# Recall of a compressive memory: blocks of 128 features in fp32, or heads of 18 features as float16 pairs through DRAM

## The chip, the cores and the metric

The kernel runs on one core of a Trainium2 chip. A core has five engines that work side by side, each through its own queue of instructions in order: TensorE (PE, the matrix products, with its weight loads shown as PEld), VectorE (DVE), ScalarE (ACT), GpSimd (POOL) and SyncE (SP), which here issues every transfer (DMA). Data lie in SBUF (128 partitions), products are summed in eight banks of PSUM, and DRAM is reached by DMA alone. The metric is the device time of one execution in microseconds.

## The reference

A sequence of 2048 tokens of 576 features is cut into four segments of 512. Each of 32 heads has 18 features. A segment attends to itself causally, and it reads a memory M (18x18 for each head) with a sum z of the segments before it; phi is 1 + t above zero and exp(t) below. The result is mixed with a GEGLU network of 4608 hidden features.

```python
for s in range(N):
    logits = jnp.einsum("bhqd,bhkd->bhqk", qs, ks) * scale + mask
    a_dot = jnp.einsum("bhqk,bhkd->bhqd", _softmax(logits, axis=-1), vs)
    pq = phi(qs)
    num = jnp.einsum("bhld,bhde->bhle", pq, M)
    den = jnp.einsum("bhld,bhd->bhl", pq, z)[..., None] + 1e-6
    outs.append(g * (num / den) + (1.0 - g) * a_dot)
    pk = phi(ks)
    M = M + jnp.einsum("bhld,bhle->bhde", pk, vs)
    z = z + jnp.einsum("bhld->bhd", pk)
...
b = (_gelu(x @ w_gate) * (x @ w_up)) @ w_down
return sigmoid((x * gate_w).sum(-1)) * (o @ wo) + (1 - sigmoid(...)) * b
```

## The kernel before

Almost every product is done with float16 pairs: a number is split into a high word and the rest, a low word, and the product is the sum of high x high, high x low and low x high.

The first 210 us hold the projections and the memory, and the rest the network, the attention and the output. The loop at the end of the function's first part runs over four segments `s`. For `s` above 0 it begins with a **rows stage**: for each of four blocks `q` of 128 tokens two products make the values (`vrows`), `key_rows` turns the key features of the segment before (`p = s - 1`), `memorize` adds them to the memory in PSUM banks U and pv, and, from `p = 1` on, `recall(p, q)` reads the memory. Then come nine **products** `j` (`project`, 14 matmuls of 512 columns each): `j` 0 to 3 and half of 4 are queries, the rest keys. The results lie in banks dn (j = 0), st (two of them, j = 1, 2, 5, 6), U (3, 7) and G (4, 8); a bank is free again when ACT and DVE have read it, and the next product for that bank waits for that. `put_columns` writes the words of `j` one product later: ACT makes the high word (`stage`), a relu and an exp, DVE the low word and the other half of phi, POOL their sum, into `phi[s, j]`.

Recall before the change: five fp32 matmuls, one for each block of 128 features, against `bd`, an fp32 block matrix of the memory that has the heads on its diagonal; a head that lies across two blocks has two parts, which `put_recall` adds. `keep_memory(p)`, at j = 1, scales the memory in PSUM and masks it into `bd`. For the last segment the recalls come after products 6, 7 and 8.

Beside the products of segments 0 to 2 runs `next_x`: ACT squares the next segment's x, POOL and DVE add the squares, and at product `XJ` (5, 5, 4) `scale_x` has PE sum them over the partitions (`norm_x`); from this DVE makes the scale `xsc`, POOL the products of scales `al`, `nal`, `esc` (`outscale`), ACT the high words of x (`high_x`, products 5 to 7) and DVE the low ones (`low_x`, 6 to 8). The next rows stage begins with them. `form_sums` makes sums of x for the network.

The order of PE, ACT, DVE and POOL is that in which the program is written. `later` collects the second half of a step, which `finish_later` writes out after the product. SP's order is set by the compiler, and each of its transfers waits in line: a transfer that is not ready holds all behind it.

## Time and profile before

| | us |
|---|---|
| runs | 1557.70, 1557.97, 2040.06 |
| median | 1557.97 |
| the profiled execution | 1557.72 |
| its span, first to last instruction | 1555.6 |
| its granted TensorE clock | 1.00 |

A page of the profile gives the busy time of each engine, its share of the span in 40 slices, the DMA queues, the chain of work that ended last (followed back from the last instruction to what released it), and the costliest groups of instructions. A row of the timeline has the start in us, the duration in us of one instruction or of several merged (x10), the engine, the line, the operation, what it writes and reads with its shape, and in brackets the idle time before it and what ended that. Durations overlap on PE: the time that a group takes is the distance to the next start.

### The profile page before, as it was taken

The page shows a single profiled execution, that of the slowest core. Times are in us where ns is not written, and L with a number is a line of the kernel's source. Part 1 is how long each engine was busy: PE and PEld are TensorE (multiplying, and loading weights), DVE is VectorE, ACT ScalarE, POOL GpSimd, SP SyncE. Part 2 cuts the span into 40 slices and gives each one's busy share as a digit, 9 for nine tenths or more (in the row PEclk, how much of TensorE's full clock was granted, in tenths as well). Part 3 has the DMA queues.
Part 4 walks back from the last instruction along what each step waited for, and adds up shares of the span by engine and source line. Part 5 has one row for each costly group of instructions (what it writes and reads, how often), then busy time and mean ns, then how long its engine had stood idle before and what let it go on. Part 6 is the DMA issues. An engine that isn't in the chain of part 4 may idle for free.

```text
span 1555.6 us, 33618 instructions
## 1 busy us (share of the span) xinstructions
PE 1549.6 (100%) x12196; PEld 951.2 (61%) x12196; DVE 1263.4 (81%) x3255; ACT 1206.8 (78%) x2059; POOL 1129.0 (73%) x1219
## 2 busy tenths in 40 slices
PE   9999999999999999999999999999999999999999
PEld 5765755565656666656656565666656666656577
DVE  7878986878888888878788888888888888887665
ACT  7667544888888888888888888888888888887421
POOL 4354566768787868686877878786868687787597
PEclk9999999999999999999999999999999999999999
DMA  7744451555657576666656675757666665664635
GB/s 244 238 153 143 153 143 39 118 124 120 155 113 148 125 154 135 143 132 130 148 123 137 120 152 119 145 127 154 137 144 137 130 156 120 141 111 103 126 83 174
DMA packets 490966, 213.77 MB, mean 137 GB/s; under 512 B 427824, under 2 KB 469808, under 8 KB 490288
## 3 DMA queue, kind: packets, MB, share of 16 engines
q1 hardware_dynamic: 490800, 211.64, 59.8%
q8 instruction: 95, 1.56, 0.4%
q14 instruction: 71, 0.58, 0.1%
HBM read 90.99 MB, written 31.98 MB: 79 GB/s over the span
## 4 chain that ended last, share of the span: by engine, by line
PE 91%; POOL 4%; DMA 1%; DVE 1%; ACT 1%; SPq 0%; issue 0%; POOLq 0%; ACTq 0%
PE dn L1259 25%; PE U L531 17%; PE G L531 12%; PE V L531 6%; PE V L1379 5%; PE pv L1212 4%; PE st L412 3%; PE dn L419 2%; PE U L1305 2%; PE G L412 1%; PE U L412 1%; PE V L1310 1%; PE st L1174 1%; PE G L1310 1%; PE G L1305 1%; PE V L1305 1%
## 5 line engine op out<-in xcount | busy, mean ns | idle before, releaser
L531 PEld LDWEIGHTS <-pairg 128*128 128x128 f16 x2592 | 247.6, 98 | 257.3 <-issue 9.8
L1195 POOL TENSOR_TENSOR pl<-pb,ph 128x896 f16<-128x896 f32 (+1 forms) x128 | 185.7, 1472 | 211.5 <-ACT ph L1194 211.5
L1259 PE MATMUL dn<-paird,hhr 128*128 128x288 f16 x2115 | 328.8, 286 | 0.2 <-DVE acc L1267 0.2
L1193 ACT ACTIVATE pb<-pb,mb,esc 128x512 f32<-128x512 f32 (+3 forms) x512 | 304.9, 642 | 5.2
L1267 DVE SCALAR_TENSOR_TENSOR acc<-dn,ev,acc 128x288 f32<-128x288 f32 x533 | 262.7, 513 | 39.2 <-PE dn L1259 33.3
L1259 PEld LDWEIGHTS <-hhr 128*128 128x128 f16 x2160 | 206.8, 98 | 78.7 <-issue 11.8
L531 PE MATMUL G<-x,pairg 128*128 128x512 f16 x864 | 210.0, 379 | 0.2 <-DVE gl L1282 0.2
L531 PE MATMUL U<-xt,pairg 128*128 128x512 f16 x864 | 209.9, 379 | 0.0
L1259 PE MATMUL dn<-paird,hhd 128*128 128x288 f16 x1275 | 209.9, 286 | 0.0
L1195 POOL TENSOR_TENSOR pb<-pb,ph 128x896 f16<-128x896 f32 (+1 forms) x128 | 179.4, 1401 | 33.3 <-ACT ph L1194 27.7
L1194 ACT ACTIVATE ph<-pb 128x896 f16<-128x896 f32 (+1 forms) x256 | 188.6, 737 | 9.7
L345 POOL TENSOR_TENSOR pairg<-raw,pairg 128x384 f16<-128x384 f32 (+2 forms) x144 | 157.6, 1116 | 16.8 <-ACT pairg L341 16.8
L1177 DVE CUSTOM_DVE_ANT_0 pb<-st,mask 128x512 f32<-128x512 f32 (+1 forms) x256 | 157.3, 614 | 0.0
L1259 PEld LDWEIGHTS <-hhd 128*128 128x128 f16 x1296 | 123.8, 98 | 50.5 <-issue 6.5
L1177 DVE CUSTOM_DVE_ANT_0 pb<-dn,mask 128x256 f32<-128x256 f32 (+1 forms) x192 | 67.2, 375 | 64.6 <-PE dn L1174 62.9
L1379 PE MATMUL V<-xt,nest 128*128 128x256 f16 x714 | 105.5, 272 | 0.0
L531 PE MATMUL U<-x,pairg 128*128 128x512 f16 x432 | 105.0, 379 | 0.0
L531 PE MATMUL V<-x,pairg 128*128 128x512 f16 x426 | 103.8, 379 | 0.1
L1300 ACT ACTIVATE gl<-gl,sc 128x512 f32<-128x512 f32 x110 | 75.8, 715 | 34.1 <-DVE gl L1571 22.3
L1212 PEld LDWEIGHTS <-pt 128*128 128x128 f16 x2560 | 80.8, 96 | 13.2 <-issue 8.4
L1297 POOL TENSOR_TENSOR hhr<-gl,hhr 128x512 f16<-128x512 f32 x64 | 79.1, 1242 | 10.8 <-ACT hhr L1289 10.7
L1212 PE MATMUL pv<-vt,pt 128*128 128x37 f16 x2560 | 85.0, 179 | 0.0
(364 smaller groups left out, 3150.9 us busy)
## 6 DMA issues: line engine op xcount, KB each, us to landing
qkt<-qk SPq DMA_DIRECT2D x256, 108.0 KB
raw<-in_wgu_dram SPq DMA_DIRECT2D x36, 640.0 KB
rawd<-in_wd_dram SPq DMA_DIRECT2D x36, 288.0 KB
qk<-stage SPq DMA_DIRECT2D x32, 256.0 KB
qk<-stage SPq DMA_DIRECT2D x40, 128.0 KB
vp<-vstage SPq DMA_DIRECT2D x16, 296.0 KB
vt<-vp SPq DMA_DIRECT2D x16, 296.0 KB
orow<-oa SPq DMA_DIRECT2D x16, 288.0 KB
```

Of the source, the lines that this page charges most:

```text
L345: pool.tensor_tensor(spot(f, *p, 1), raw_g[f][:, p[0] : p[1]], spot(f, *p, 0), OP.subtract)
L412: pe.matmul(o, w(k, a), x[:, i], start=n == 0, stop=n == 13, skip_group_check=True)
L531: pe.matmul(o, w[:, i, (a + k) * P : (a + k + 1) * P], x[:, b + k], start=start and k == 0 and i == 0 and b == h, stop=k == 1 and i == 1, ...
L1177: dve.tensor_tensor_reduce(scored(a, qi), out[qi], mask[:, L - (qi + 1) * P :], 1.0, -3e38, OP.add, OP.max, mx[a][:, qi : qi + 1])
L1193: act.activation(r, r, AF.Exp, bias=b[:, qi : qi + 1], scale=esc[:, 0, c : c + 1])
L1194: act.activation(h[:, cols], p, AF.Copy)
L1195: pool.tensor_tensor(low[:, cols], p, h[:, cols], OP.subtract)
L1212: pe.matmul(ov, pr[:, 10 * i + COL[qi] // P + kb], v[:, 4 * e + kb, c0 : c0 + VC], start=kb == 0 and i == 0, stop=kb == qi and i == 1)
L1259: pe.matmul(o[:, :NH], hh[:, a, q * P : (q + 1) * P], w[:, b, n * NH : (n + 1) * NH], start=i == 0, stop=i == 5)
L1267: dve.scalar_tensor_tensor(av, o[:, :NH], ev, av, OP.mult, OP.add)
L1297: pool.tensor_tensor(hh[:, 1], t, hh[:, 0], OP.subtract)
L1379: pe.matmul(o, w[:, (7 * c + i) * P : (7 * c + i + 1) * P], x[d], start=start and n == 0, stop=n == 2, skip_group_check=True)
```

## The change

Recall goes by heads and with float16 pairs.

- `put_columns` scales phi by a power of two of its own (`ali`, and a bias `lnv` in the exp; the scale had been applied in `key_rows`). `split_phi` then makes a pair of each query block of 128 features: ACT copies it to float16, POOL subtracts, and SP writes it to DRAM (`phq`) as three rows for each feature, high, low, high.
- `load_phi(s, g)` reads 54 rows (18 features x 3) for each head, two heads above each other in a tile of 128 partitions, eight transfers for the eight heads of a group `g`. Three such tiles take turns.
- `recall(s, g)` goes over four blocks of tokens for one group of eight heads, where the old one went over all heads for one block: sixteen matmuls of 38 columns for five of fp32 (which run as ten).
- `keep_memory` masks in PSUM, adds the blocks of a head up into `mc`, and sums segments there. `memory_pairs`, new at j = 2, squares the memory on ACT, sums over the partitions on PE, makes a scale by the norm, forms pairs on POOL and ACT, and sends them through DRAM (`md`) into `mpair`, two heads of 54 rows beside each other in 38 columns. The recall's result is brought back by `ghs` and `eps`.
- The memory's blocks hold seven heads (126 features) in place of eight; the last holds four.
- `key_scale` moves from the rows stage to product 2 (segment 0) and behind `outscale` in `next_x`. Three subtractions of `form_sums` go from DVE to POOL. For the last segment the recalls still follow products 6, 7 and 8, one to each, and the last one the end.

```diff
+        def split_phi():
+            while phis:
+                s, j, f = phis.pop(0)
+                m = min(P, D - j * P)
+                st = pp.tile([P, 2, L], F16, name="stage", bufs=5)
+                act.activation(st[:m, 0], f[:m], AF.Copy)
+                pool.tensor_tensor(st[:m, 1], f[:m], st[:m, 0], OP.subtract)
+                r = phq[s - 1][j * P : j * P + m]
+                sp.dma_start(r[:, :2], st[:m])
+                sp.dma_start(r[:, 2], st[:m, 0])
+
+        def load_phi(s, g):
+            r = phq[s - 1].rearrange("f a t -> (f a) t")
+            n = 3 * DH
+            for i in range(2):
+                t = phg[s, g, i] = pp.tile([P, 2, L], F16, name="phg", bufs=3)
+                for e in range(2):
+                    for k in range(2):
+                        o = (8 * g + 4 * i + 2 * k + e) * n
+                        sp.dma_start(t[64 * e : 64 * e + 64, k], r[o : o + 64])
...
-                act.activation(e, e, AF.Exp, scale=-1.0)
+                act.activation(e, e, AF.Exp, bias=lnv[:, s : s + 1], scale=-1.0)
+            split_phi()
+            if j <= 4 and s >= 1:
+                phis.append((s, j, f))
...
-        def recall(s, q, banks=(("st", 2), ("st", 2))):
...
-                pe.matmul(o[:, (h0 - lo) * MC : (h1 - lo) * MC], phi[s, j][:, q * P : (q + 1) * P],
-                          bd[:, j, : (h1 - h0) * MC], start=j in (0, 3), stop=j in (2, 4), skip_group_check=True)
+        def recall(s, g, banks=(("st", 2), ("st", 2))):
+
+            o = [bank(*i) for i in banks]
+            for i in range(2):
+                t = phg.pop((s, g, i))
+                for q in range(4):
+                    for k in range(2):
+                        c = (q % 2) * 8 * MC + (2 * i + k) * 2 * MC
+                        pe.matmul(o[q // 2][:, c : c + 2 * MC], t[:, k, q * P : (q + 1) * P], mpair[:, 4 * g + 2 * i + k],
+                                  start=i == k == q % 2 == 0, stop=i == k == q % 2 == 1, skip_group_check=True)
+            later.append(lambda: put_recall(s, g, o))
...
+        def memory_pairs(s):
+            q = pp.tile([P, 2], F32, name="msq", bufs=1)
+            for i, c in enumerate((slice(0, DH), slice(DH, MC))):
+                act.activation(m16[:, :, 2, c], mc[:, :, c], AF.Square, accum_out=q[:, i : i + 1])
+            o = sums(q, bank("dn", 2))
...
+            act.activation(m16[:, :, 0], mt, AF.Copy)
+            act.activation(m16[:, :, 1], m16[:, :, 0], AF.Copy)
+            pool.tensor_tensor(m16[:, :, 2], mt, m16[:, :, 0], OP.subtract)
...
+            sp.dma_start(md[: 4 * MT].rearrange("(j p) a c -> p j a c", p=MT), m16[:MT, :4])
+            sp.dma_start(md[4 * MT :], m16[: D - 4 * MT, 4])
...
+                sp.dma_start(mpair[64 * e : 64 * e + n, :, e * MC : (e + 1) * MC], r[e])
...
         def key_scale(s):
...
+            dve.tensor_scalar(lnv[:, s : s + 1], iv.bitcast(I32), 1065353216.0, LN2 * 2.0**-23, OP.subtract, OP.mult)
+            pool.tensor_scalar(ali[:, s], al[:, s, 0:3:2], iv, None, OP.mult)
...
                     for i in range(3):
                         outscale(c, i)
+                    key_scale(c)
...
                         if p >= 1:
                             recall(p, q)
+                            if q < 3:
+                                load_phi(p, q + 1)
...
+                    if s and j == 2:
+                        memory_pairs(p)
...
+                    if s and j == 6:
+                        load_phi(s, 0)
+                    if s == 3 and j > 5:
+                        recall(3, j - 6, (("V",), ("pv",)) if j == 7 else (("dn", 2), ("dn", 2)))
+                        load_phi(3, j - 5)
```

The first place is POOL's queue in the products of segment 1. The 128x512 phi rows are the sums of phi, `pairg` the additions of the squares of x, `al` the scales. Before:

```order
L664 TENSOR_TENSOR phi<-phi,expm 128x512
L164 TENSOR_TENSOR pairg<-pairg 128x512 x2
L664 TENSOR_TENSOR phi<-phi,expm 128x512
L164 TENSOR_TENSOR pairg<-pairg 128x512 x2
L664 TENSOR_TENSOR phi<-phi,expm 128x512 x2
L123 TENSOR_SCALAR al<-wis,xis 128x1
```

Now, from the end of the memory's pairs (`eps` is their last instruction):

```order
L845 TENSOR_SCALAR eps<-mu,kmc 128x1
L166 TENSOR_TENSOR pairg<-pairg 128x512 x2
L698 TENSOR_TENSOR phi<-phi,expm 128x512
L664 TENSOR_TENSOR stage<-phi,stage 128x512
L166 TENSOR_TENSOR pairg<-pairg 128x512 x2
L698 TENSOR_TENSOR phi<-phi,expm 128x512
L664 TENSOR_TENSOR stage<-phi,stage 128x512
L698 TENSOR_TENSOR phi<-phi,expm 128x512
L664 TENSOR_TENSOR stage<-phi,stage 128x512
L125 TENSOR_SCALAR al<-wis,xis 128x1
```

A subtraction for the pair of each block stands behind the sum of that block (each behind its copy on ACT), and the pairs of the memory ahead of all.

The second place is DVE's queue behind the norm's matmul of segment 1 (`kmc` is written by `key_scale`, which reads `al`). Before:

```order
L193 TENSOR_SCALAR xis<-xv 128x1
L663 TENSOR_SCALAR phi<-G,al 128x512
L669 SCALAR_TENSOR_TENSOR stage<-G,stage 128x512
L216 SCALAR_TENSOR_TENSOR x_1149<-raw,xsc,x_1149 128x1024
L663 TENSOR_SCALAR phi<-st,al 128x512
```

Now:

```order
L195 TENSOR_SCALAR xis<-xv 128x1
L855 TENSOR_SCALAR kmc<-al 128x1
L856 TENSOR_SCALAR kmc<-kmc 128x1
L857 TENSOR_SCALAR lnv<-kmc 128x1
L697 TENSOR_SCALAR phi<-G,ali 128x512
L703 SCALAR_TENSOR_TENSOR stage<-G,stage 128x512
L218 SCALAR_TENSOR_TENSOR x_1217<-raw,xsc,x_1217 128x1024
```

The three instructions of `key_scale` now stand ahead of the reading of bank G and of the low words of x.

The third place is SP's queue in the products of segment 3 (`qk` takes the words of a product, `phq_68` the pairs of phi, `phg` is what the recalls read). Before, `om<-mo` is the result of a recall:

```order
L675 DMA qk<-stage 64x512
L674 DMA qk<-stage 64x2x512 x2
L675 DMA qk<-stage 128x512
L674 DMA qk<-stage 128x2x512
L675 DMA qk<-stage 128x512
L747 DMA om<-mo 128x576 x2
```

Now:

```order
L709 DMA qk<-stage 64x512
L666 DMA phq_68<-stage 64x1024
L667 DMA phq_68<-stage 64x512
L708 DMA qk<-stage 128x2x512
L709 DMA qk<-stage 128x512
L677 DMA phg<-phq_68 64x512 x14
L778 DMA om<-mo 128x4x144
L708 DMA qk<-stage 128x2x512
L709 DMA qk<-stage 128x512
L677 DMA phg<-phq_68 64x512 x8
```

Six of the eight loads of the first group stand behind the writes of the last block of phi and the words of product 5; the other eight of the fourteen are those of the second group.

More of the change, by code (lines that the diff above doesn't have):

```diff
@@ L33 @@
 LN256 = 5.545177444479562
+LN2 = 0.6931471805599453
 NEG = -1e30
@@ L38 @@
 SPANS = [(128 * j, min(128, D - 128 * j)) for j in range(KT)]
-HS = 21
-HEADS = [(a // DH, (a + w - 1) // DH + 1) for a, w in SPANS]
+MT = 7 * DH
+MSPANS = [(MT * j, min(MT, D - MT * j)) for j in range(KT)]
+HEADS = [(a // DH, (a + w) // DH) for a, w in MSPANS]
 @with_exitstack
@@ L491, in last_sum @@
         dve.scalar_tensor_tensor(flat(x[:, 4:6]), r[2, 1], sc, flat(x[:, 0:2]), OP.mult, OP.subtract)
+    phq = [dram.tile([D + 4, 3, L], F16, name=f"phq{i}", bufs=1) for i in range(3)]
+    md = dram.tile([D, 3, MC], F16, name="md", bufs=1)
     qks, vps, oms, oas = [], [], [], []
@@ L510 @@
     esc = cst.tile([P, 2, 4], F32, name="esc")
-    kmc = cst.tile([P, 3, 4], F32, name="kmc")
+    kmc = cst.tile([P, 4, 4], F32, name="kmc")
     gha = cst.tile([P, 4, H], F32, name="gha")
@@ L715, in first_words @@
                           start=k == 0, stop=k == 4)
-        def recall(s, q, banks=(("st", 2), ("st", 2))):
-            na, nb = (bank(*i) for i in banks)
-            for j, (h0, h1) in enumerate(HEADS):
-                o, lo = (na, 0) if j < 3 else (nb, HS)
-                pe.matmul(o[:, (h0 - lo) * MC : (h1 - lo) * MC], phi[s, j][:, q * P : (q + 1) * P],
-                          bd[:, j, : (h1 - h0) * MC], start=j in (0, 3), stop=j in (2, 4), skip_group_check=True)
-            later.append(lambda: put_recall(s, q, na, nb))
@@ new lines, in keep_memory @@
+            for o, k, d in ((ka[:, : 3 * n], flat(bdm[:, 0:3]), t[:, 0:3]), (kb[:, :n], bdm[:, 3], t[:, 3:4]),
+                            (kb[:r, n : n + m], bdm[:r, 4, :m], t[:r, 4:5])):
+                dve.scalar_tensor_tensor(o, o, sm[: o.shape[0]], k, OP.mult, OP.mult)
+                v = o.rearrange("p (j h d) -> p j d h", j=d.shape[1], d=MC)
+                dve.tensor_reduce(d, v, AX.X, OP.add)
+            dve.tensor_scalar(t[:, :, DH:], t[:, :, DH:], zf, 2.0**-15, OP.mult, OP.mult)
@@ L860 @@
             first_words(va, 0, 4, range(4))
-            x1 = [pp.tile([P, L], F32, name="phi", bufs=9) for _ in range(2)]
+            x1 = [pp.tile([P, L], F32, name="phi", bufs=6) for _ in range(2)]
             for i, t in enumerate(x1):
@@ L933, in behind_rows @@
             def behind_rows(s, q):
+                if s == 2 and q < 3:
+                    form_sums(0, q, -1, pool)
                 if s == 3:
@@ L976, in beside_products @@
                         x_raw.pop(0)
+                    if j == 2:
+                        key_scale(0)
                     if j == 4:
```

111 lines of the change are left out of this document (57 added, 54 removed).

## The prediction

> **What bounds the kernel now.** I read the page first, for the engine that is full and the chain that ended last.
>
> ```profile
> PE 1549.6 (100%) x12196; PEld 951.2 (61%) x12196; DVE 1263.4 (81%) x3255; ACT 1206.8 (78%) x2059; POOL 1129.0 (73%) x1219
> ...
> PE 91%; POOL 4%; DMA 1%; DVE 1%; ACT 1%; SPq 0%; issue 0%; POOLq 0%; ACTq 0%
> ```
>
> TensorE (PE) is busy for 1549.6 of 1555.6 us and carries 91% of the chain. So PE work taken out is time won, and every microsecond in which PE is made to wait is time lost. The change lies wholly in the first 210 us, so I cut these into stages with a view of stretches (columns: PE, weight loads, DVE, ACT, POOL, the clock, DMA share, GB/s).
>
> ```profile
> 72.00:100.00 28.00, 28.00 (x142) 13.17 (x140) 18.78 (x39) 19.58 (x35) 16.97 (x21) 1.00 0.38 108
> 100.00:125.00 25.00, 25.00 (x226) 21.81 (x225) 23.34 (x62) 12.91 (x25) 6.47 (x8) 1.00 0.48 167
> 125.00:152.00 27.00, 27.00 (x137) 12.80 (x136) 23.20 (x44) 20.91 (x35) 14.54 (x18) 1.00 0.44 136
> 152.00:177.00 25.00, 25.00 (x228) 21.80 (x227) 22.75 (x65) 12.27 (x29) 10.18 (x14) 1.00 0.47 164
> 177.00:210.00 33.00, 33.00 (x182) 18.35 (x181) 32.07 (x69) 23.49 (x44) 24.59 (x25) 1.00 0.53 167
> ```
>
> The first, third and fifth rows are the nine products of segments 1, 2 and 3; the second and fourth are the rows stages between. PE never rests. In the products ACT has some 6 to 10 us to spare, POOL 8 to 12, DVE almost nothing in segment 3: that is the cover under which new work would have to go.
>
> **What PE wins.** The timeline of PE gives the old recall and the product into the memory, and a later group of 128x37 products the price of small ones.
>
> ```profile
> 103.47 1.37 PE L723 MATMUL st<-bd,phi 128*128 128x152 f32 x10
> 104.68 1.63 PE L419 MATMUL U<-wv,x 128*128 128x288 f16 x12
> ...
> 109.99 0.81 PE L777 MATMUL U<-vstage,krow 128*128 128x152 f16 x9
> ...
> 110.95 1.64 PE L419 MATMUL dn<-wv,x 128*128 128x288 f16 x12
> ```
>
> ```profile
> 707.17 0.68 PE L1212 MATMUL pv<-vt,pt 128*128 128x37 f16 x20
> 707.70 0.49 PE L1379 MATMUL V<-xt,nest 128*128 128x256 f16 x3
> ```
>
> From start to next start a recall takes 1.21 us, and twenty products of 37 columns 0.53 us, 26.5 ns each. Sixteen of 38 columns take 0.42. Twelve recalls win 12 x 0.79 = 9.5 us. The product into the memory takes 0.96 us for 2016 columns and now has 1792 (seven heads for eight): 0.11 us, twelve times 1.3. Three tiny sums cost about 0.1. The win is 10.7 us: 3.4 if a small product cost what one into the memory costs, 0.96 / 15 = 64 ns, and 12.2 if it went by columns alone, 18 ns; I take the row of nearly the same shape.
>
> **What lies beside.** The old put_recall had nine DVE instructions and the new has seven; DVE waits for PE in the rows stages, so I count nothing. Three subtractions of the input sums go from DVE to POOL in the rows stage of segment 2, where POOL is busy for 6.47 of 25 us: nothing, while that stays so. The new traffic, 1.8 MB out and 2.1 MB in for each segment, meets a DMA share of 0.38 to 0.53: nothing, unless transfers queue. The 38-byte pieces of the memory's load have no row; in segment 3 they leave SP some 6 us before they are used, so they are covered up to that.
>
> **What PE has to wait for.** Per query column block there is now an ACT copy and a POOL subtraction, and the next copy waits for the next POOL sum: three engines' queues are tied to each other. Prices of the same forms:
>
> ```profile
> L1297 POOL TENSOR_TENSOR hhr<-gl,hhr 128x512 f16<-128x512 f32 x64 | 79.1, 1242 | 10.8 <-ACT hhr L1289 10.7
> ...
> L1289 ACT ACTIVATE hhr<-gl 128x512 f16<-128x512 f32 x64 | 38.5, 615 | 10.3 <-DVE gl L1282 10.2
> ```
>
> A sum (1.27 below), copy 0.62 and subtraction 1.24 give 3.2 us a block with the handovers, against 3.02 us of PE for a product. Nothing that is late here is made up. I now walk segment 1 through the new order with the durations of this timeline.
>
> ```profile
> 75.52 0.25 DVE L787 TENSOR_SCALAR U<-U,kmc 128x24 f32<-128x24 f32 x1 [1.02 <-PE U L777]
> ...
> 77.07 0.73 DVE L663 TENSOR_SCALAR phi<-dn,al 128x512 f32<-128x512 f32 x1
> ...
> 77.95 1.27 POOL L664 TENSOR_TENSOR phi<-phi,expm 128x512 f32<-128x512 f32 x1 [2.80 <-DVE phi L663]
> ...
> 78.86 0.69 ACT L653 ACTIVATE stage<-st,unq 128x512 f16<-128x512 f32 x1 [2.06 <-PE st L412]
> ...
> 80.69 1.65 ACT L157 ACTIVATE pairg<-raw 128x512 bf16<-128x512 f32 x3
> ...
> 81.68 3.19 PE L412 MATMUL U<-x,wp 128*128 128x512 f16 x14
> 81.90 2.38 POOL L164 TENSOR_TENSOR pairg<-pairg 128x512 bf16<-128x512 bf16 x2 [2.67 <-ACT pairg L157]
> ...
> 85.47 2.39 POOL L164 TENSOR_TENSOR pairg<-pairg 128x512 bf16<-128x512 bf16 x2
> ...
> 90.75 0.38 PE L176 MATMUL dn<-pairg,onesb 128*128 128x512 bf16 x1
> ```
>
> ```profile
> 92.64 1.15 ACT L199 ACTIVATE x<-raw,xsc 128x1024 f16<-128x1024 f32 x1 [2.17 <-DVE xsc L192]
> ...
> 92.76 0.29 POOL L123 TENSOR_SCALAR al<-wis,xis 128x1 f32<-128x1 f32 x1 [2.46 <-DVE xis L193]
> ...
> 93.84 1.28 DVE L216 SCALAR_TENSOR_TENSOR x<-raw,xsc,x 128x1024 f16<-128x1024 f32 x1
> ...
> 100.03 1.63 PE L419 MATMUL dn<-wv,x 128*128 128x288 f16 x12
> ```
>
> The new keep_memory has seven DVE instructions from 75.5 on; between the shortest (0.25) and the longest row (0.73) they take 1.8 to 5.1 us; I take 2.8, since four work on 19 to 133 elements. So the first phi is on DVE at 78.3 (77.07 before) and its POOL sum ends at 80.35. ACT's three steps of a block end at 80.7; copy to 81.3; the two squares with their accumulators to 82.2 (estimate). PE, free at 81.7, waits **0.6** for them. PE's sum, three small DVE and three POOL instructions end at 84.15; ACT stands still for that, converts until 84.8, squares the input until 86.45, and POOL's first additions end at 88.35 (84.28 before). Sum of block 1 to 89.6, copy to 90.3, subtraction to 91.55; then the other additions, 2.4 us, until 93.95. The norm's matmul (90.75 before, with its data since 87.86) would be ready at 91.55 and waits **2.5**. POOL goes on: sum 95.2, copy, subtraction 97.15, sum 98.4, copy, subtraction 100.4, and only then al, at 100.7 instead of 93.05. DVE stands at key_scale for that al; behind it are block 4's phi and words, done at 102.8, and until then bank G is taken: product 8, due at 100.2, waits **2.6**. ACT's copy of block 4 comes after POOL's sum at 104.15, so the last high words of x come at 108.6 and the last low ones at 109.6; the rows stage has used all else by 107.3 and waits **2.3**. Segment 1: 8.0 us (0 if all fits into slack; 11 if each handover costs a quarter more).
>
> Segment 2 the same way, shifted to its rows:
>
> ```profile
> 134.20 3.19 PE L412 MATMUL U<-x,wp 128*128 128x512 f16 x14
> ...
> 140.25 0.38 PE L176 MATMUL V<-pairg,onesb 128*128 128x512 bf16 x1
> ...
> 152.55 1.63 PE L419 MATMUL dn<-wv,x 128*128 128x288 f16 x12
> ```
>
> The squares end at 136.4, and PE, free at 134.2, waits 2.2 (DVE has a 1.27 us conversion of x ahead of the first phi). The norm's additions end at 147.5 and PE waits 1.9; al comes at 151.0, bank U is free at 153.0, 2.2 more; the last words of x at 163.4, 3.0 more. Together **9.3 us**.
>
> Segment 3 has no next x, but its loads stand in line on SP.
>
> ```profile
> 186.17 1.26 POOL L664 TENSOR_TENSOR phi<-phi,expm 128x512 f32<-128x512 f32 x1
> ...
> 186.84 3.19 PE L412 MATMUL U<-x,wp 128*128 128x512 f16 x14
> ...
> 198.93 1.37 PE L723 MATMUL dn<-bd,phi 128*128 128x152 f32 x10
> ...
> 208.65 1.38 PE L723 MATMUL st<-bd,phi 128*128 128x152 f32 x10
> ```
>
> ```profile
> 107.16 0.32 SPq L747 DMA_DIRECT2D om<-mo  x1
> ```
>
> ```profile
> 1552.33 0.52 DVE L1744 SCALAR_TENSOR_TENSOR acc<-st,gate,acc 128x288 f32<-128x288 f32 x1 [0.46 <-PE st L1740]
> ```
>
> The last DVE result is ready at 1552.85 and the span ends at 1555.6: issue and landing of a transfer take 2.75 us, 2.4 behind the issue. The Trainium skill (DMA: Bandwidth & Descriptors, section Anatomy of one DMA — SWDGE (gpsimd) path) puts the fixed part of a transfer at about 2.0 us; by it each of the six waits for a load below would be 0.4 us shorter, estimated from that page, and the forecast 1582.6; the row is of this kernel, and I keep it. POOL's first sum ends at 187.45 as before, the squares at 189.0: PE waits **2.2** and, four products of 3.02 later, reaches the first recall at 201.3. The chain sum, copy, subtraction runs on until 206.6 for block 4. On SP the rest of the loads of heads 0 to 7 stand behind the writes of that block and the words of block 5: ten issues, 3.4 us, and 2.4 to land, 212.4. The first recall waits **11.1**. The next ones reload tiles that the one before has just read, four issues and a landing, 3.7 us, against 3.02 us of product, and behind put_recall's store: 0.2, 1.4 and 2.0. Together **16.9 us** (2 if the loads go out early; 22 with slower landings). In the two rows stages the second group's loads stand behind the last words of block 8: 1.1 and 2.7, **3.8 us**.
>
> **The sum.** 8.0 + 9.3 + 3.8 + 16.9 = 38.0 us of waits, less 10.7: +27.3. The profiled execution took 1557.7 us, 1555.6 of span and 2.1 around it, and the median of the runs shown is 1558.0, the same within 0.3. 1557.7 + 27.3 = **1585.0 us**. After 210 us the order of every engine is as before, and PE is full, so nothing gives it back.
>
> **Rivals.** (1) *Not slower: the waits are covered.* If the copies and subtractions find their places in the 8 to 12 us that POOL has free, only the win is left: 1547. It decides at 3.02 us a block, and my 3.2 is above it by little; but the memory's chain alone puts 5 us ahead of it. 7%. (2) *SP is no line.* If the loads land before their recalls, 14.7 and 3.8 go: 1566.5. For it: SP is mostly idle in the rows stages; against it: the order of the queue. 16%. (3) *The x path holds.* If al and the last words come in time as before (7.4 us ahead, 92.64 to 100.03), the 17.3 of segments 1 and 2 go: 1567.7. 14%. (4) *It costs more than the sum of the parts.* DVE and POOL stretch each other where both read SBUF:
>
> ```profile
> 144.60 3.48 POOL L664 TENSOR_TENSOR phi<-phi,expm 128x512 f32<-128x512 f32 x2
> 144.72 2.22 DVE L216 SCALAR_TENSOR_TENSOR x<-raw,xsc,x 128x1024 f16<-128x1024 f32 x1
> ```
>
> The DVE instruction took 1.28 alone, the POOL sum 1.27 and here 1.74. Two more such stretches of 0.94 in each of two segments are 3.8 us. And if PE ran at half its clock for the product after the 11 us wait, that product would take 3 us more: 1585 + 6.8 = 1591.8. 27%. The Trainium skill (GPSIMD Engine Reference, section Specifications) says that POOL shares its SBUF interfaces with DVE and that they contend where DVE has two SBUF inputs; by that rule the stretch is certain, and these two rows agree with it. The Trainium skill (TensorE: Matmul & The Clock Gate, section What's actually happening) says that after an idle window of about 3.4 us the clock drops to half; the granted clock is 1.00 in all five stretches, PE never rests there, and no run here shows it.
>
> **How the numbers follow.** The forecast as summed has 36%, the rivals 7, 16, 14 and 27. The range 1558 to 1602 takes in (2), (3), (4) and the forecast; it leaves out (1) and some of what (4) could grow to with slow landings. 2% of 1558 is 31 us, about what a measurement of this kernel can tell from no change: slower begins at 1589. Three quarters of (4) and 30% of the forecast lie above, 31%; faster by 2% would take more than PE can win, 1%; the rest, 68%, is within.
>
> **What would show it.** In the changed profile: a recall of 0.4 to 0.5 us on PE (the win); PE's wait for ACT before a matmul of two columns in each product 3; al on POOL later by some 8 us against the norm's matmul, DVE idle before key_scale, and PE waiting for DVE at products 7 or 8; PE waiting for a DMA before the first recall of segment 3 by about 11 us. If PE is still at 100% of the first 210 us, I am wrong by the whole 38; if it waits in segment 3 alone, (3) is right.

## The result and the profile after

| | us |
|---|---|
| before, median of 5 runs | 1557.7 |
| after, median of 5 runs (1613.97 to 1617.98) | 1616.58 |
| ratio, with its 95% interval | 1.0376 (1.0364 to 1.0388) |
| the profiled execution, its span | 1616.1, 1614.1 |
| its granted TensorE clock | 0.986 |

The change makes the kernel 58.9 us slower; 27.3 were forecast, and the time lies above the range. The page of the kernel after, busy times and chain of work that ended last:

```profile
PE 1557.5 (96%) x12271; PEld 944.9 (59%) x12271; DVE 1262.4 (78%) x3245; ACT 1217.8 (75%) x2092; POOL 1164.0 (72%) x1264
...
PE 82%; POOL 6%; ACT 3%; DVE 3%; DMA 3%; SPq 2%; issue 2%; POOLq 0%; ACTq 0%; DVEq 0%
```

PE was busy for all but 6 us of its span before, and now rests for 56.6 us; its busy time, which should have gone down by 10.7 us, has gone up by 7.9. The view of stretches, cut at the same places as before (first product to rows stage of segment 1, rows stage 2, segment 2, rows stage 3, segment 3 with the first product of the network; columns as before: length, PE, weight loads, DVE, ACT, POOL, clock, DMA share, GB/s):

```profile
72.74:106.27 33.53, 30.46 (x145) 13.74 (x143) 17.36 (x45) 19.56 (x39) 21.57 (x31) 0.95 0.42 127
106.27:137.96 31.69, 23.47 (x246) 18.61 (x245) 25.86 (x53) 16.21 (x31) 15.86 (x13) 0.95 0.58 174
137.96:174.23 36.27, 30.18 (x145) 13.65 (x143) 20.33 (x47) 23.13 (x43) 21.93 (x30) 0.95 0.54 164
174.23:206.22 31.99, 23.55 (x248) 18.67 (x247) 25.11 (x63) 14.19 (x33) 11.89 (x15) 0.95 0.74 233
206.22:265.05 58.83, 36.25 (x214) 16.83 (x212) 30.70 (x64) 28.45 (x55) 34.17 (x37) 0.80 0.56 164
```

Before, the same stages took 28.4, 24.1, 28.4, 24.2 and 33.1 us: the loss is 5.2, 7.6, 7.9, 7.8 and 25.7 us, with 1.1 at the start and 3.3 after 265 us. No stage is shorter. The last cut is not quite at the same place: six matmuls of the network's next product (L535, 2.5 us) stand ahead of it in this kernel and behind it before, though the program writes them later. The compiler's order on PE is not always that of the program. What PE waited for in these stages, from the view of waits (us in total, times, the longest):

```profile
PE dn L759 <- DMA phg<-phq: 18.0, 8, 12.3
PE st L759 <- DMA phg<-phq: 6.5, 10, 1.5
PE V L178 <- POOL pairg L166: 4.9, 1, 4.9
PE dn L423 <- DVE x L223: 3.9, 2, 2.0
PE dn L96 <- ACT nest L91: 3.5, 1, 3.5
PE dn L178 <- POOL pairg L166: 2.8, 1, 2.8
PE G L535 <- DVE stage L703: 2.4, 1, 2.4
PE dn L421 <- DVE x L218: 2.3, 2, 2.1
PE dn L96 <- ACT m L829: 2.3, 2, 1.1
...
PE dn L421 <- ACT x L201: 0.6, 1, 0.6
```

Half of it, 24.5 us, are recalls (L759) that wait for their loads. 14.5 us belong to the path of the next x: its norm (L178) and its last words (L421, L423). One row is new in kind: 3.5 us before the small matmul of the network's weight statistics (L96). Its cause stands in the timeline of rows stage 3, four engines deep (DVE, SP, ACT and PE in turn):

```profile
168.97 1.28 DVE L218 SCALAR_TENSOR_TENSOR x<-raw,xsc,x 128x1024 f16<-128x1024 f32 x1 [2.12 <-ACT x L201]
```

```profile
175.00 1.75 SPq L677 DMA_DIRECT2D phg<-phq  x3
...
177.95 1.41 SPq L243 DMA_DIRECT2D raw<-in_wgu_dram  x3
```

```profile
182.16 0.74 ACT L595 ACTIVATE krow<-raw 128x640 bf16<-128x640 f32 x1 [2.70 <-DMA raw<-in_wgu_dram]
```

```profile
186.64 0.17 PE L96 MATMUL dn<-stat,onesb 128*128 128x10 bf16 x1 [3.45 <-ACT nest L91]
```

The network's first weights are loaded into the raw buffers that the words of x set free. The first is free at 170.25, its load leaves at 177.95, on SP behind the writes of the features' last block, writes of words and the recall's loads; ACT's squares and PE wait for it. Two causes are possible, the late x and SP's line; experiments 9 and 10 part them.

The clock is new too. Behind the wait of 2.78 us for the norm the next product, 3.02 us long at full speed, took 4.70 (rows of PE, segment 1):

```profile
94.91 0.38 PE L178 MATMUL dn<-pairg,onesb 128*128 128x512 bf16 x1 [2.78 <-POOL pairg L166]
95.13 4.87 PE L414 MATMUL st<-x,wp 128*128 128x512 f16 x14
99.83 3.19 PE L414 MATMUL U<-x,wp 128*128 128x512 f16 x14
103.25 3.18 PE L414 MATMUL G<-x,wp 128*128 128x512 f16 x14 [0.23 <-DVE stage L703]
```

In slices of 1 us the granted clock is 0.50 from 96 to 98 us, and again behind five other waits; from the busy time in these slices the slow stretches hold 13.8 us that full speed would not have taken. Whether that lengthens the kernel is asked of the third experiment.

### The profile page after: what moved, and what is told of

It reads as the page before. It is cut to its first block, busy times and chain, and to the rows that moved or that the text cites. A ratio compares the mean times of both kernels' runs of the same rounds, so it can differ in the third digit from the quotient of the medians.

```text
span 1614.1 us, 34082 instructions
## 1 busy us (share of the span) xinstructions
PE 1557.5 (96%) x12271; PEld 944.9 (59%) x12271; DVE 1262.4 (78%) x3245; ACT 1217.8 (75%) x2092; POOL 1164.0 (72%) x1264
## 4 chain that ended last, share of the span: by engine, by line
PE 82%; POOL 6%; ACT 3%; DVE 3%; DMA 3%; SPq 2%; issue 2%; POOLq 0%; ACTq 0%; DVEq 0%
PE dn L1326 25%; PE U L535 17%; PE G L535 11%; PE V L535 6%; PE V L1446 5%; PE pv L1279 4%; PE U L1372 2%; SPq L677 1%; PE V L1377 1%; PE G L1377 1%; PE st L1241 1%; PE V L1372 1%; PE G L1372 1%; POOL phi L698 1%; PE dn L421 1%
## 5 line engine op out<-in xcount | busy, mean ns | idle before, releaser
L535 PEld LDWEIGHTS <-pairg 128*128 128x128 f16 x2592 | 248.2, 98 | 262.5 <-issue 17.1
L535 PE MATMUL G<-x,pairg 128*128 128x512 f16 x864 | 211.2, 381 | 2.6 <-DVE stage L703 2.4
L535 PE MATMUL U<-xt,pairg 128*128 128x512 f16 x864 | 210.3, 379 | 0.0
L1262 POOL TENSOR_TENSOR pb<-pb,ph 128x896 f16<-128x896 f32 (+1 forms) x128 | 179.6, 1403 | 33.8 <-ACT ph L1261 27.8
L1367 ACT ACTIVATE gl<-gl,sc 128x512 f32<-128x512 f32 x110 | 75.8, 715 | 46.7 <-DVE gl L1602 24.2
L535 PE MATMUL V<-x,pairg 128*128 128x512 f16 x426 | 105.0, 383 | 0.9 <-DVE gl L554 0.8
L535 PE MATMUL U<-x,pairg 128*128 128x512 f16 x432 | 105.0, 379 | 0.0
L414 PEld LDWEIGHTS <-wp 128*128 128x128 f16 x504 | 49.5, 100 | 73.9 <-issue 19.5
L1364 POOL TENSOR_TENSOR hhr<-gl,hhr 128x512 f16<-128x512 f32 x64 | 79.7, 1251 | 10.7 <-ACT hhr L1356 10.6
```

The costliest lines, as they stand in the source:

```text
L535: pe.matmul(o, w[:, i, (a + k) * P : (a + k + 1) * P], x[:, b + k], start=start and k == 0 and i == 0 and b == h, stop=k == 1 and i == 1, ...
L1262: pool.tensor_tensor(low[:, cols], p, h[:, cols], OP.subtract)
L1364: pool.tensor_tensor(hh[:, 1], t, hh[:, 0], OP.subtract)
L1367: act.activation(t, o, AF.Gelu_apprx_tanh, scale=scl[f // 2][0][:, 2 + c : 3 + c])
```

## The experiments

Times are medians; the runs of before beside them gave 1557.4 to 1557.9 us. Where a stage's length is given, it is the distance between the starts of the same matmuls as above. Three causes were in view, each with a price of its own: (a) the copies and subtractions of the features make the path of x late; (b) the loads stand in SP's line; (c) half clock after the waits.

**1. The subtraction on DVE.**

```diff
-                pool.tensor_tensor(st[:m, 1], f[:m], st[:m, 0], OP.subtract)
+                dve.tensor_tensor(st[:m, 1], f[:m], st[:m, 0], OP.subtract)
```

> The five subtractions of split_phi in each segment go from POOL to DVE. Theory (POOL's chain is late): POOL's sum, copy, subtraction put the additions of the input norm and the scales al some 7 to 9 us late; with the subtraction on DVE the waits for the norm (2.8 in segment 1, 4.9 in segment 2) fall below 1.5 each, those for the last words of x (6.8 in both) to 3 or less, the 4.2 us wait for the network's weight statistics in rows stage 3 (its raw buffers are freed by the words of x) below 1, and with them the stretches at half clock that follow: about 1598 us, 19 below the 1616.6 of the changed kernel. Rival (only the engine changes that all wait for): DVE stands at the copy of ACT with the next phi and the low words of x behind it, so the same waits come back: 1612 to 1620.

1613.3 us (ratio 1.0341 to 1.0372): the rival. DVE now makes the scale of x later than before, as these rows of DVE show: the subtraction (L664) stands ahead of the norm (L179), and waits for ACT's copy.

```profile
99.49 0.69 DVE L664 TENSOR_TENSOR stage<-phi,stage 128x512 f16<-128x512 f32 x1 [1.48 <-ACT stage L663]
100.10 0.68 DVE L179 TENSOR_REDUCE x<-dn 128x1 f32<-128x512 f32 x1
```

In the kernel after, L179 ran at 95.33. POOL is free, and the same time is lost one queue further on.

**2. Half as many loads.**

```diff
-                    for k in range(2):
-                        o = (8 * g + 4 * i + 2 * k + e) * n
-                        sp.dma_start(t[64 * e : 64 * e + 64, k], r[o : o + 64])
+                    sp.dma_start(t[64 * e : 64 * e + n], r[o : o + 4 * n].rearrange("(k e p) t -> e p k t", k=2, e=2)[e])
```

The tiles that the loads write also become three named buffers, set to zero at the start.

> A load of a tile of two heads takes one transfer of 54 rows x 2 for each half in place of two of 64 rows: 4 in place of 8 for each group, the same rows. Theory (SP pays for each transfer, 0.63 us in a row of them): the 24.5 us that PE waits for these loads fall to about 10, and the half clock behind the long one stays: 1600 to 1604 us. Rival (SP pays by the bytes or rows, or the loads wait for their data): a transfer takes twice as long, and the time stays at 1613 to 1620.

1603.7 us (1.0281 to 1.0311), 13.0 us won. A group's loads in a row, on SP, after and here:

```profile
122.60 5.10 SPq L677 DMA_DIRECT2D phg<-phq  x8
```

```profile
120.25 2.46 SPq L677 DMA_DIRECT2D phg<-phq  x4
```

Eight issues take 5.1 us, 0.64 each; the forecast had 0.34. Four of 108 KB each, for 64 KB, take 2.5 here (1.8 to 4.5 in other places). The waits for loads fall from 24.5 to 13.6 us, rows stage 3 from 32.0 to 29.1 and segment 3 from 58.8 to 53.3. Cause (b) holds, and the first recall of segment 3 still waits 11.1.

**3. PE kept busy in its waits.**

```diff
+        def warm(o, n):
+            for _ in range(n):
+                pe.matmul(o, W[8][:, 0, :P], W[8][:, 0, :512], start=True, stop=True)
...
+            if s == 3:
+                warm(o[1], (52, 0, 16, 0)[g])
```

> Matmuls whose result is thrown away fill some of PE's idle time: 9 before the norm of segment 1, 19 before that of segment 2, 18 before rows stage 2, 11 before the weight statistics, 52 and 16 before the first and third recall of segment 3; all shorter than the wait they stand in. Theory (half clock after the waits costs by itself, 13.8 us in six stretches): the waits end at the same events, the granted clock stays 1.00, and the time is 1604 to 1607 us. Rival (in segment 3 PE is held by the loads anyway): there the time won turns into longer waits, only the four stretches ahead of it are won, 6.4 us: 1610. Second rival (the clock is no cost, the waits are all): 1616 to 1619.

1617.1 us (1.0365 to 1.0400): the second rival. The product behind the norm now takes 3.01 us, and the time comes back two products later (rows of PE; L182 is the norm, L422 the product):

```profile
95.08 0.38 PE L182 MATMUL dn<-pairg,onesb 128*128 128x512 bf16 x1 [0.81 <-POOL pairg L166]
95.30 3.18 PE L422 MATMUL st<-x,wp 128*128 128x512 f16 x14
98.31 3.19 PE L422 MATMUL U<-x,wp 128*128 128x512 f16 x14
103.42 3.18 PE L422 MATMUL G<-x,wp 128*128 128x512 f16 x14 [1.92 <-DVE stage L713]
```

Product 8 starts at 103.42, after at 103.25. It waits for bank G, which DVE frees when POOL's al has come; here the other engines set its start, whatever PE's clock. So at this place the half clock is a sign of the waits and no price of its own.

The experiment does not show this for all six stretches. It left 7.6 of the 13.8 us of half clock, in part at new places, and the compiler gave SP another order too: a recall in rows stage 2 now waits 4.6 us for its load. Behind the last recall, where PE waits for little else, the same matmuls took longer at half clock. From L549 to L96 they took 8.6 us in the kernel after, and 5.5 here (L557 is L549 there; rows of PE, after first):

```profile
265.05 2.73 PE L549 MATMUL V<-xt,hhr 128*128 128x512 f16 x6
...
273.66 0.17 PE L96 MATMUL dn<-stat,onesb 128*128 128x10 bf16 x1
```

```profile
269.81 1.60 PE L557 MATMUL V<-xt,hhr 128*128 128x512 f16 x6
...
275.32 0.17 PE L96 MATMUL dn<-stat,onesb 128*128 128x10 bf16 x1
```

That place alone costs the kernel after about 3 us. The equal times of the two kernels are a gain there and later loads elsewhere. How much of the 13.8 us is a price of its own is not shown.

**4. Recalls of segment 3 that wait for no load.**

```diff
                 t = phg.pop((s, g, i))
+                if s == 3:
+                    t = x16[3][:, 2 * i : 2 * i + 2]
```

> The recalls of segment 3 read words of x in place of the loaded features (the last segment's recall is not computed); its loads still go out. Theory (the loads' line on SP is what segment 3 waits for): the 12.3, 1.5, 0.2, 2.2 and about 1.5 us of waits go, with 7 us of half clock: 1592 to 1596 us. Rival (the waits are taken over by what is late anyway: PE's banks through DVE, the first products of the network): a loss of less than 12, 1605 or more.

1603.1 us (1.0276 to 1.0306), between the two. The five waits went, and PE then stood 11.2 us at the network's first product, for a bank that DVE had to read. DVE and SP at that place:

```profile
251.60 0.82 DVE L777 TENSOR_TENSOR mo<-dn,rden 128x288 f32<-128x288 f32 x2 [9.30 <-DMA om<-mo]
```

```profile
239.95 8.79 SPq L677 DMA_DIRECT2D phg<-phq  x14
248.84 0.53 SPq L780 DMA_DIRECT2D om<-mo  x1
```

The third result needs a buffer mo, its store stands behind fourteen loads, and DVE behind it. So in this kernel SP's line holds PE by two ways, the loads and the stores. In the kernel after DVE waits for no store. Its 2.4 us at bank G come from DVE reading the bank at 259.86, behind the results of a recall for whose matmuls DVE had waited 4.70 us. The same wait is 1.9 us in experiment 13, where no recall waits for a load.

**5 and 6. Copy and subtraction one step later**, behind the x path of the same product: on POOL, and (with the line of the first experiment) on DVE.

```diff
                     beside_products(s, j)
+                    split_phi(j - 2)
```

> split_phi (copy, subtraction, writes) is written one step later: behind the x path of the same product (squares, additions, al, words of x), and not ahead of it. Theory (the order of the queues makes the x path late: ACT's copy waits for POOL's sum with the words of x behind it, POOL's subtraction stands ahead of the norm's additions and of al): the segment times from first product to rows stage fall from 33.5 and 36.3 to about 30 and 31 us, rows stage 3 from 32.0 to 28 because the raw buffers come free in time; 1605 us. Rival (POOL is full: nine sums at 1.27, five subtractions at 1.16, four additions at 1.2, some 6 us of small ones are 28 us of 28.4): what is taken from one place is missing at the next, 1612 to 1618.

> As before it, split_phi one step later, behind the product's own DVE steps, and its subtraction on DVE. Theory (order of the queues): like the late one on POOL or better, 1602 to 1605 us, since POOL also loses 5.8 us a segment. If POOL's load was the bound and not the order, this one wins and the late one on POOL does not: 1602 against 1615. Rival (DVE stands at ACT's copy as in the first experiment): 1612 or more.

On POOL 1624.6 us (1.0414 to 1.0445), worse; on DVE 1611.1 (1.0325 to 1.0360). Segment 1 becomes shorter in both (31.6 and 31.1 for 33.5), as theory (a) says; but the features are written later, and the recalls wait longer: on POOL rows stage 2 goes from 31.7 to 35.5 us and segment 3 from 58.8 to 65.1, with an idle time of PE of 19.2 us before its first recall. Block 4's subtraction ran 34.5 us behind the start of that segment, for 29.9 after, and the loads behind it left at 246.4. The two chains bite into each other: what one gives up, the other takes.

**7. The first loads of segment 3 two products earlier**, with the loads of experiment 2.

```diff
-                    if s and j == 6:
+                    if s and j == (4 if s == 3 else 6):
                         load_phi(s, 0)
```

> One transfer for each half tile (as in the second experiment), and the first group's loads of segment 3 are written two products earlier (at j = 4), which puts them in SP's line ahead of the writes of blocks 3 and 4. Theory (the first recall waits for its place in SP's line, not for data): the wait of 11.1 us falls below 1.5, segment 3 from 53.3 to about 43 us, and the time from 1603.7 to 1592 to 1594. Rival (the line only moves on: the later groups' loads still stand behind put_recall's store and the last words): the wait goes to the second and third recall and 1600 or more is left.

1601.1 us (1.0264 to 1.0294): by the medians 2.6 less than experiment 2, in place of 10 to 12, and with intervals that overlap. The stage tells more: segment 3 took 50.6 us, for 53.3. PE's rows of that recall:

```profile
232.05 0.37 PE L759 MATMUL dn<-mpair,phg 128*128 128x38 f16 x8 [3.14 <-DMA phg<-phq]
234.84 0.41 PE L759 MATMUL dn<-mpair,phg 128*128 128x38 f16 x8 [2.42 <-DMA phg<-phq]
```

This recall's waits, 11.9 us in experiment 2, became 5.6, so the place in line was half of them. What the rest is made of, the way of the features through the engines or SP again, which here issues without a gap from 222.4 to 230.4, is not shown. The later recalls got new waits of 1.6 and 1.7 us. **8.** Five and seven together:

> Both changes together: split_phi late on POOL, one transfer for each half tile, the first group's loads two products earlier. If the two causes are separate, their gains add: 1580 to 1585 us. If one cover takes in both (POOL full, or SP's pace), about the better one alone: 1590 to 1595.

1602.1 us (1.0269 to 1.0300): nothing more than seven alone.

**9 to 13. Parts left out.** Copy and subtraction; all transfers of the features; the memory's transfers; the first two; and these with the memory's pairs as well. Of the lines below, the first three are of 9, the others of 10. Eleven leaves out the four transfers of the memory's pairs, and 13 the body of `memory_pairs`.

```diff
-                act.activation(st[:m, 0], f[:m], AF.Copy)
-                pool.tensor_tensor(st[:m, 1], f[:m], st[:m, 0], OP.subtract)
+                st = f
...
-                sp.dma_start(r[:, :2], st[:m])
-                sp.dma_start(r[:, 2], st[:m, 0])
...
-                t = phg.pop((s, g, i))
+                t = W[8]
```

> ACT's copy and POOL's subtraction of split_phi are left out, with their stage tiles: SP writes the words of the queries to DRAM in their place (the recall is then of other data); all transfers, loads and recalls stay. Theory (these ten instructions a segment, each in line with the x path, make x late): first product to rows stage falls from 33.5 and 36.3 to about 30 and 31 us, the wait for the weight statistics goes with its cause, and segment 3's writes leave some 3 us earlier: about 1600 us. Rival (the memory's chain of squares, norm, pairs and its transfers makes x and the writes late): 1610 or more.

> The writes and loads of the features (96 loads, 30 writes) are left out; the recalls read words of a weight in SBUF in their place. Copy, subtraction and the memory's own transfers stay. Theory (SP's line): PE's waits for loads, 24.5 us, go with the 2.4 us behind them, segment 3 from 58.8 to 36 us, the rows stages from 31.7 and 32.0 to 28 and 29, while the segments' first parts stay at 33 and 36: 1583 to 1587 us. Rival (without the loads PE stands at the next late thing, such as the last copy and subtraction or the memory's load): 1595 or more.

> The memory's four transfers (md and back into mpair) are left out of each segment, and the recall reads a memory of zeros. Theory (mpair stands in SP's line until md has landed, and the features' writes of block 1 stand behind it, 9.7 us after those of block 0): these writes leave some 5 us earlier, 3 to 5 us of the first recall's wait go, and 1610 to 1613 us are left. Rival (the line is set by the loads' own pace): 1615 to 1618.

> Copy, subtraction, writes and loads of the features are all left out; the memory's new work, the power of two in phi, the new recall and product into the memory stay. Theory (the features' pairs and their way through DRAM are the whole loss): the 10.7 us forecast for PE show, less some 5 us of waits for the memory's norm: 1551 to 1556 us. Rival (the memory's chain is a large part itself): 1562 or more.

> Against the run without the features' pairs and transfers (1563.9 us): the memory's norm, pairs and transfers are left out as well (the recall reads a memory of zeros). Theory (their steps stand on ACT, PE, DVE and POOL ahead of the norm of x): first product to rows stage goes from 29.2 and 33.1 to 28.4 and 29 us with the wait of 3.0 and the half clock behind it gone: 1558 to 1560 us. Rival (the norm of segment 2 is late by the work on the input sums at its start): segment 2 stays above 32, 1562 or more.

| left out | us | ratio, 95% | segment 1 | rows 2 | segment 2 | rows 3 | segment 3 |
|---|---|---|---|---|---|---|---|
| before the change | 1557.7 | | 28.4 | 24.1 | 28.4 | 24.2 | 33.1 |
| nothing (after) | 1616.6 | 1.0364 to 1.0388 | 33.5 | 31.7 | 36.3 | 32.0 | 58.8 |
| 9: copy, subtraction | 1599.1 | 1.0247 to 1.0281 | 29.2 | 28.9 | 33.1 | 29.8 | 55.1 |
| 10: transfers of features | 1587.8 | 1.0178 to 1.0208 | 33.5 | 29.8 | 37.5 | 23.3 | 34.9 |
| 11: transfers of memory | 1612.3 | 1.0337 to 1.0368 | 33.5 | 31.2 | 37.4 | 32.0 | 57.7 |
| 12: 9 and 10 | 1563.9 | 1.0025 to 1.0051 | 29.2 | 24.1 | 33.1 | 21.8 | 30.9 |
| 13: 12 and the memory's pairs | 1555.3 | 0.9975 to 0.9994 | 28.3 | 23.7 | 28.3 | 22.1 | 30.4 |

Nine came out in time as its theory had it, though segment 2 stayed at 33.1 for 31, and the wait for the weight statistics stayed too, 3.4 us, where x was no longer late. In ten x was as late as ever and that wait was gone: the first weights left SP at 168.37, when their buffer came free (168.34). So it belongs to SP's line. Ten is 1 us above its theory. Eleven has the time that was expected, but its interval overlaps that of the kernel after, so no gain is clear, and it has not the way: the first recall's wait stayed at 12.3 us, so the memory's place in SP's line is not what that wait is made of. Twelve gave the rival: the memory's chain is a part of its own. Thirteen shows it: segment 2 goes from 33.1 to 28.3 us, as before the change. (Segment 3 of the kernel after, 9 and 11 contains the network's six matmuls named above; before, 10, 12 and 13 do not.) Read from the last row up, the four parts are a staircase:

| part | step | us |
|---|---|---|
| the shorter recall and product, with nothing of what feeds them | before to 13 | -2.5 |
| the memory's norm, pairs and transfers | 13 to 12 | +8.7 |
| copy and subtraction of the features | 12 to 10 | +23.9 |
| their transfers | 10 to after | +28.8 |
| sum | | +58.9 |

Taken off in the other order the transfers cost 35.2 (12 to 9) and copy and subtraction 17.5 (9 to after): 6.4 us belong to both. The first step also holds the other small changes, among them the new `key_scale` and `keep_memory` and the subtractions moved to POOL, and every step holds what the compiler orders otherwise on PE and SP.

**14 and 16. Rows stage 2**, on the basis of 12: two DVE instructions of the recall left out, and the subtractions of the input sums on DVE again.

```diff
-            dve.reciprocal(flat(rd), flat(dn))
-            dve.tensor_tensor(rd, rd, sc[:, 8 * g : 8 * g + 8].unsqueeze(1).to_broadcast([P, 4, 8]), OP.mult)
+            rd = nil
```

```diff
-                if s == 2 and q < 3:
-                    form_sums(0, q, -1, pool)
...
-                        form_sums(0, q - 1, 2)
+                        form_sums(0, q - 1, 0)
```

> Against 1563.9 us: DVE's reciprocal and its product with the scale are left out of put_recall (the recall becomes zero). Theory (DVE sets rows stage 2, since that small product with two operands in SBUF takes 1.55, 2.05 and 2.04 us in place of 0.19 while POOL subtracts the input sums): rows stage 2 goes from 24.1 to about 22, the waits for krow (2.9) with it: 1561 to 1562 us. Rival (PE sets it): 24, and 1563 to 1565.

> Against 1563.9 us: the three subtractions of the input sums are on DVE again, as before the change. Theory (on POOL they cost DVE 1.4 to 1.9 us each, by the product that takes 2 us beside them; on DVE they cost 1.22 each): DVE gains some 1.4 us, rows stage 2 goes from 24.1 to 22.7 us, and the time to 1562 to 1563. Rival (DVE is stretched by something else): rows stage 2 becomes longer by up to 3.7 us, 1565 to 1568.

14 gave 1561.3 us (1.0016 to 1.0034) and a rows stage 2 of 21.7 us. 16 gave 1563.2 (1.0021 to 1.0047), 23.6 there and 1.2 more in segment 2. Both are right in direction in that stage, and too small to be told in the time: their intervals overlap that of 12. In 12 that stage looks so (stretch; then one product of DVE, and POOL beside it):

```profile
101.86:126.00 24.14, 21.50 (x247) 17.75 (x246) 23.66 (x49) 12.51 (x26) 13.65 (x12) 1.00 0.51 168
```

```profile
112.94 2.05 DVE L768 TENSOR_TENSOR rden<-rden,ghs 128x32 f32<-128x32 f32 x1
```

```profile
112.58 2.36 POOL L447 TENSOR_TENSOR acc<-acc 128x1024 f32<-128x1024 f32 x1
```

And the same product in 16, where POOL has no subtraction beside it:

```profile
113.02 0.19 DVE L768 TENSOR_TENSOR rden<-rden,ghs 128x32 f32<-128x32 f32 x1
```

DVE is busy for 23.66 of 24.14 us: it has become the bound of that stage, which takes 2.4 us less when two of its instructions go (14).

**15. What helped, together:** the loads of 2 and 7; in segments 1 and 2 the subtraction late and on DVE, and the first loads there behind those of the weights (at j = 8).

> A whole kernel that computes all: one transfer for each half tile, the first loads of segment 3 two products earlier, in segments 1 and 2 the subtraction late and on DVE, and there the first loads behind those of the network's weights. If the causes are separate and add: 1616.6 - 15.5 (transfers and place) - 5.5 (late on DVE) - some 4 (weight statistics): 1590 to 1594 us. If they cover each other: 1597 to 1602.

1594.4 us (1.0225 to 1.0255), the time at the upper end of what the theory of separate causes gave, but not in its way. Rows stage 3 took 33.8 us, longer than after, with one wait for the recall's loads that now stand behind the weights:

```profile
180.60 0.41 PE L760 MATMUL st<-mpair,phg 128*128 128x38 f16 x8 [9.33 <-DMA phg<-phq]
```

It is the best whole kernel here, 22 us faster than the change and 37 slower than before. With the features for nothing the times are 1563.9 and 1555.3 (12 and 13); no order of feeding this recall that was tried comes near them.

## Why the prediction was wrong

The side was right, the mechanisms were right in kind, and the sum was less than half. Three steps failed: DVE was counted for nothing in the rows stages, the loads were given too fast a pace behind too short a chain, and, outside rival (4), PE's products behind waits were priced at full clock. Term by term, with PE's own waits in the kernel after and what the same part cost when it was left out (which is more than its waits, and so not the same thing; 2.2 us of waits lie outside these stages):

| term | forecast | PE's waits, after | by parts left out |
|---|---|---|---|
| PE's win | -10.7 | | -2.5 |
| waits for the memory's norm (0.6, 2.2, 2.2) | 5.0 | 2.3 | 8.7 |
| x path in segments 1 and 2 (8.0 and 9.3 less 0.6 and 2.2) | 14.5 | 14.8 | 17.5 to 23.9 |
| loads and SP (3.8, and 16.9 less 2.2) | 18.5 | 24.5 | 28.8 to 35.2 |
| not in the forecast: weights' statistics 3.5, gate 0.8, bank G 2.4 | 0 | 6.7 | |

The spans give the whole: PE rests 50.6 us more than before, for 38.0 forecast, and is busy for 7.9 more, for 10.7 less forecast. So of the 31 us that the forecast misses, 12.6 are waits and 18.6 are busy time. The win itself is not what failed there: in 13, where the clock is 1.00, PE is busy for 9.7 us less than before.

```profile
PE 1539.9 (99%) x12268; PEld 939.5 (60%) x12268; DVE 1261.4 (81%) x3236; ACT 1207.3 (78%) x2059; POOL 1136.9 (73%) x1229
```

The kernel after is busy for 17.6 us more than that: 13.8 are the half clock, and 3.8 are not traced. That busy time is not all price, as experiment 3 shows; how much of it is stays open.

- **"The win is 10.7 us."** The price was right: the first recall takes 0.41 us from its start to the next matmul (0.42 forecast), a product into the memory 0.85. The step that failed is the sentence that DVE waits for PE in the rows stages and so counts for nothing. It was busy for 23.34 of 25 us there, a row that the prediction showed. In 13 new waits of 7.3 us take most of the 9.7 back, and 3.6 of them are waits for DVE, most in rows stage 2; that stage stayed at 24.1 us in 12 and went to 21.7 when DVE lost two instructions (14). The others are 1.9 us for bank G at the network's start, 1.4 for an ACT exponential at the first rows stage and small ones. So DVE is about half of what is missing from the win.
- **"Three subtractions go to POOL: nothing."** DVE's small product then took 2.05 us for 0.19 beside them (12, 16), and with the subtractions back on DVE that stage was 0.6 us shorter. The stretch of DVE and POOL stood in the prediction as rival (4) and was priced there with 0.94 us a time, in another place.
- **The x path.** Segment 1 came as walked through: the norm's matmul waited 2.78 us (2.5 forecast), and al was there at 101.38 (100.7, on a time scale on which the segment starts 1.1 us earlier). But PE got the last words of x at 112.8, or 111.7 on that scale (109.6), and waited 4.6 us for words where 2.3 were forecast. The wait for bank G, 2.6 in the forecast, is 0.23 in the profile: the product ahead ran at half clock and had used it up, as experiment 3 shows, where it is 1.92. In segment 2 the norm's wait was 4.95 and not 1.9. The three kinds of wait, for the norm, the banks and the words, are 7.7, 0.2 and 6.8 us in both segments, for 4.4, 4.8 and 5.3 forecast: that their sum agrees is luck. Rival (3), that this path holds, is refuted by 9. What was mis-sized in segment 1 are the last steps: behind al stand eight more small instructions on POOL, so that its sum of block 4, which ACT's copy waits for, ended 4.6 us behind al, at 105.97, for 3.4 forecast, and DVE's low words took 2.46 us for 1.28, beside a subtraction and a sum of POOL (rows of POOL, the last beside that instruction, and of DVE):

```profile
101.07 0.31 POOL L125 TENSOR_SCALAR al<-wis,xis 128x1 f32<-128x1 f32 x1
...
104.71 1.26 POOL L698 TENSOR_TENSOR phi<-phi,expm 128x512 f32<-128x512 f32 x1
...
107.82 1.26 POOL L698 TENSOR_TENSOR phi<-phi,expm 128x512 f32<-128x512 f32 x1
```

```profile
107.70 2.46 DVE L218 SCALAR_TENSOR_TENSOR x<-raw,xsc,x 128x1024 f16<-128x1024 f32 x1 [2.05 <-ACT x L201]
```

- **SP.** The first wait in segment 3 was 12.3 us (11.1 forecast), the step that rested on the order of the queue. Two sizes failed in it. The chain of sum, copy and subtraction ended block 4 at 237.28, 7.6 us behind PE's arrival and not 5.3; POOL's sums took up to 2.29 us for 1.27 there. And the pace, "ten issues, 3.4 us", was too fast: eight loads took 5.0 to 6.4 us and fourteen 8.8. So the recall's second half began 14.8 us behind PE's arrival, where 11.1 were forecast for all its loads; that the first wait came so near is partly luck, since the recall's first half needed only some of the loads. The later ones waited 4.5 us (3.6) and those of the rows stages 5.5 (3.8). One more thing behind the line was not seen: the network's weights, 3.5 us (10). Rival (2), SP no line, is refuted by 2 and 10.
- **Rival (1)**, that the waits are covered, is refuted by the result itself.
- **Rival (4)** named the half clock and priced it at 3 us. It came six times and not once. The product behind the 12.3 us wait took 4.8 us, 1.8 more than at full clock. A product that runs slowly between two waits for other engines only shortens the second one (3, segment 1); behind the last recall, with little waiting behind it, it cost about 3 us. The Trainium skill (TensorE: Matmul & The Clock Gate, section What's actually happening) has the clock fall after an idle window of about 3.4 us; here a wait of 2.78 us was enough, and the measurement decides.
- **"After 210 us nothing gives it back"** held: nothing came back, and the part behind 265 us is 3.3 us longer, most of it in slow matmuls and a wait of 0.8 us before 274 us.

The Trainium skill (GPSIMD Engine Reference, section Specifications) says that DVE with two operands in SBUF and POOL contend for an interface; experiments 12 and 16 agree, with 2.05 against 0.19 us.

What stays open: why a load of 64 rows in a row of eight takes SP 0.63 to 0.80 us, when one of 54 x 2 rows takes 0.45 to 1.13 in experiment 2 and 0.38 to 1.16 in experiment 7. That there are fewer of them helps is shown; what sets the pace is not. Open too are what the half clock costs in all, and the 3.8 us of busy time that are not traced.

## What to carry to other kernels

Where the engine that is full gets less to do, look for the next one in that very stage: a DVE at 23.3 of 25 us is the new bound, and took about half of what was missing from the win. A step that goes through three engines and DRAM costs what its queues hold up behind it, also on buffers that someone else waits for (raw here, mo in experiment 4); follow the buffers as well as the results. And leave parts out one after the other before mending orders: the staircase of five kernels told more than six attempts to move a step.

## What the runs showed of the hardware

- A DVE product of 128x32 with two operands in SBUF takes 0.19 us alone and ended each time with POOL's subtraction beside it: 112.94 + 2.05 against 112.58 + 2.36, and twice more, at 109.72 against 109.68 and 121.43 against 121.39 (12).
- The granted clock fell to 0.50 behind a wait of 2.78 us, for some 3.5 us of work. Whether that lengthens the kernel depends on what follows: nothing at product 8 of segment 1, about 3 us behind the last recall of segment 3.
- Eight loads of 64 rows (64 KB each) leave SP in 5.0 to 6.4 us, four of 54 x 2 rows (108 KB) in 1.5 to 4.6 (2, 7).
- A queue of transfers in line also holds up what has nothing to do with it: a store behind fourteen loads held a buffer and DVE for 9.3 us (4), and a weight load left 7.7 us after its buffer was free (after).
